# The last 512 weight columns of two heads loaded in unequal row groups

## The chip, the cores and the metric

The kernel runs on one core of one Trainium2 chip. The metric is the device time of one execution in microseconds (us). The core has the engines TensorE (PE), VectorE (DVE), ScalarE (ACT), GpSimd (POOL) and SyncE (SP), and 16 DMA engines, which carry all loads. TensorE's weight loads stand apart in the profile as PEld.

## The reference

Two layers, each an attention step over a key and value cache and a gated feed-forward, run twice with the same weights and caches. All is float32; two batch rows, one token each.

```python
def _A_ref(x, k_cache, v_cache, wq, wo):          # H 16, Sk 4096, Dh 256, D 448
    q = (x @ wq).reshape(B, Sq, H, Dh).transpose(0, 2, 1, 3)
    scores = jnp.einsum("bhqd,bhkd->bhqk", q, k_cache) * (Dh ** -0.5)
    p = _softmax(scores, axis=-1)
    o = jnp.einsum("bhqk,bhkd->bhqd", p, v_cache)
    return o.transpose(0, 2, 1, 3).reshape(B, Sq, H * Dh) @ wo
def _B_ref(x, W_gate, W_up, W_down):              # F 1792
    gate = jnp.einsum("bsd,df->bsf", x, W_gate)
    gate = gate * (gate > 0)
    return jnp.einsum("bsf,fd->bsd", gate * jnp.einsum("bsd,df->bsf", x, W_up), W_down)
x = x + _A_ref(_layernorm(x), ...); x = x + _B_ref(_layernorm(x), ...)
x = x + _A_ref(_layernorm(x), ...); x = x + _B_ref(_layernorm(x), ...)
```

## The kernel before

The work is a stream of loads from HBM into one large SBUF tile, the arena, with the arithmetic fitted beside it. A unit is one head of one batch row: 32 units in each of the two passes. Keys and values of a unit lie in HBM as rows of 128 partitions; a whole block is the values of one unit and the keys of the next, 128 rows of 16384 numbers, 64 KB each (8 MB in all). Beside them go the head weights (`in_w_head_dram`): for each head 128 rows of 1792 numbers (7 KB each). Of these columns the first 896 hold the query weights, and the last 896 the output weights, in two halves of 448 that the projection multiplies one after the other. After the 32 units of a pass come the feed-forward's weights (`in_w_in_dram`, `in_w_out_dram`), likewise in rows of 7 KB, and the very last of them in narrower pieces.

`loads` writes the order of all loads by hand, first for pass 1, then for pass 2, and `pending` holds it. `pump` (called at every `release` of a buffer) takes loads from the head of that list while there is room in the arena and issues each as one DMA from SP's queue (the page's line L142). The arena has three whole blocks and three single places; a head's weights go into a single place. `query(u)` multiplies a head's first 896 columns, `project(u)` the last 896 (PE, L579), and `project` then releases the head's place, for which the next head's load waits. In pass 2 the heads come in the order 15, 14, 0, 1, ... 13, so heads 9 and 11 are loaded late in pass 2, each between two whole blocks.

In the last feed-forward, `block` (PE, L736) multiplies by `in_w_out_dram` as it arrives, and the results are copied out by ACT and DVE (L762, L769, L777) and stored by two small DMAs.

A load with 128 rows is spread over the 16 DMA engines by rows. Each engine works through its own queue in order; nothing holds one engine back for another, unless an issue waits. What SP waits for before an issue is a buffer's release, and the semaphore of the load eight issues earlier, which the new load uses again (named DMAHW0 to DMAHW7 in the program). Instructions of the five engines are fetched by the same 16 DMA engines, in packets of 16 KB (queue q8) and 8 KB (queue q14).

## Time and profile before

| | |
|---|---|
| time, median of 3 runs (range) | 1317.86 us (1317.57 to 1317.97) |
| the profiled execution's own time | 1317.97 us |
| its span, first to last instruction | 1316.1 us |
| busy share of PE, DVE, ACT, POOL | 43%, 82%, 15%, 22% |
| loads on SP's queue | 99.5% of the 16 DMA engines' span |
| moved | 561.32 MB, mean 427 GB/s |
| mean granted TensorE clock | 0.686 |

In the tables of stretches, a row gives the stretch in us from the span's start, its length, each engine's busy time with its number of instructions, the granted TensorE clock, the busy share of the 16 DMA engines (1.00 is all sixteen) and GB/s. In a list of instructions in order of time a row gives start, duration, engine, line, operation, and in brackets the idle time before it with what ended it. In the list of waits a row names who waited for whom, then us in total, times, and the longest. A list of DMA queues gives packets, MB and the time that the packets took as a share of 16 engines over the stretch.

### The profile page before, as it was taken

What the parts mean: (1) busy time and instruction counts of PE and PEld (TensorE: products, weight loads), DVE (VectorE), ACT (ScalarE), POOL (GpSimd) and SP (SyncE); (2) the same over time, 40 slices, a digit from 0 to 9 for tenths busy, and PEclk for the clock granted to TensorE, in tenths of its full rate; (3) what the DMA queues carried; (4) which work ended last, traced back from release to release, by engine and by line L of the source; (5) the groups of instructions that cost most, each with busy time, mean ns of one, the idle gap of its engine ahead of it and who ended that gap; (6) DMA issues with size and microseconds to landing.
All of it is one profiled execution on the core that took longest, in us unless ns stands there. A gap on an engine that the chain in (4) does not pass through costs nothing.

```text
span 1316.1 us, 9097 instructions
## 1 busy us (share of the span) xinstructions
PE 561.0 (43%) x3280; PEld 194.9 (15%) x3280; DVE 1082.5 (82%) x789; ACT 198.2 (15%) x779; POOL 291.4 (22%) x192
## 2 busy tenths in 40 slices
PE   2243342433424334245495544232443424424358
PEld 2011110110111101112142111010111101111113
DVE  4989888898888988788829987698898888877892
ACT  1100000010000000221016523000000000012242
POOL 0202003322133221321001153022052321130210
PEclk9676766767667676676796667666666667666569
DMA  9999999999999999999999999999999999999998
GB/s 406 438 431 426 437 427 430 439 434 429 424 443 432 431 435 419 444 423 428 422 397 402 430 428 436 440 431 428 429 441 431 428 435 435 426 434 429 428 423 333
DMA packets 22665, 561.32 MB, mean 427 GB/s; under 512 B 2520, under 2 KB 2652, under 8 KB 9948
## 3 DMA queue, kind: packets, MB, share of 16 engines
q1 hardware_dynamic: 22612, 560.74, 99.5%
q8 instruction: 26, 0.43, 0.1%
q14 instruction: 19, 0.16, 0.0%
q10 hardware_dynamic: 8, 0.00, 0.0%
HBM read 560.73 MB, written 0.00 MB: 426 GB/s over the span
## 4 chain that ended last, share of the span: by engine, by line
DMA 56%; DVE 30%; PE 8%; POOL 2%; issue 2%; ACT 1%; DVEq 0%; SPq 0%; POOLq 0%; ACTq 0%
DMA arena<-in_vk_dram 53%; DVE arena L431 12%; DVE tiny L445 11%; PE po L530 2%; DVE down L477 2%; POOL tiny L488 2%; DMA arena<-in_w_in_dram 2%; DVE arena L468 2%; DVE arena L477 2%; DMA arena<-in_w_out_dram 1%; PE small L556 1%; DVE row L546 1%; PE acc L579 1%; PE pq L377 1%; ACT arena L470 1%
## 5 line engine op out<-in xcount | busy, mean ns | idle before, releaser
L431 DVE TENSOR_TENSOR arena<-arena 128x8192 f32<-128x8192 f32 (+2 forms) x52 | 441.8, 8497 | 108.0 <-DMA arena<-in_vk_dram 107.9
L445 DVE TENSOR_REDUCE tiny<-arena 128x32 f32<-128x8192 f32 (+2 forms) x53 | 430.3, 8118 | 0.0
L556 PE MATMUL small<-tiny,row 128*128 128x1 f32 x256 | 62.0, 346 | 667.1 <-DVE row L546 667.1
L530 PE MATMUL po<-arena,tiny 128*2 128x512 f32 x2052 | 303.5, 733 | 20.4 <-ACT arena L521 10.3
L488 POOL PARTITION_ALL_REDUCE tiny<-tiny x64 | 71.0, 1109 | 625.2 <-DVE tiny L486 625.2
L502 POOL PARTITION_ALL_REDUCE tiny<-tiny x64 | 192.1, 3002 | 61.3 <-ACT tiny L496 60.3
L556 PEld LDWEIGHTS small<-tiny,row 128*128 128x128 f32 x256 | 56.6, 308 | 728.2 <-DVE row L546 728.2
L493 ACT ACTIVATE tiny<-tiny 128x1 f32<-128x1 f32 x64 | 18.8, 294 | 600.9 <-POOL tiny L488 600.9
L393 POOL PARTITION_BROADCAST arena<-arena x58 | 27.6, 545 | 296.1 <-ACT arena L389 296.1
L530 PEld LDWEIGHTS po<-arena,tiny 128*2 128x2 f32 x2052 | 55.3, 96 | 209.4 <-issue 192.3
L377 PE MATMUL pq<-arena,xs 128*33 128x256 f32 x174 | 76.8, 611 | 12.6 <-DMA arena<-in_w_head_dram 12.6
L579 PE MATMUL acc<-arena,tiny 128*2 128x448 f32 x128 | 50.2, 881 | 32.1 <-DVE tiny L569 32.1
L389 ACT ACTIVATE arena<-pq 33x256 f32<-33x256 f32 x29 | 10.9, 377 | 318.7 <-PE pq L381 318.7
L437 ACT ACTIVATE arena<-arena 128x256 f32<-128x256 f32 x104 | 41.7, 402 | 87.7 <-DVE arena L431 87.7
L546 DVE SCALAR_TENSOR_TENSOR row<-po,tiny,row 128x256 f32<-128x256 f32 x64 | 30.7, 480 | 25.8 <-ACT row L543 25.5
L470 ACT ACTIVATE arena<-arena 128x256 f32<-128x256 f32 x117 | 47.1, 404 | 20.8 <-DVE arena L468 20.5
L468 DVE TENSOR_TENSOR arena<-arena 128x1024 f32<-128x1024 f32 (+1 forms) x24 | 42.0, 1749 | 0.0
L377 PEld LDWEIGHTS pq<-arena,xs 128*33 128x33 f32 x174 | 25.7, 164 | 79.5 <-issue 65.8
L543 ACT ACTIVATE row<-po,tiny 128x256 f32<-128x256 f32 x64 | 29.2, 456 | 27.3 <-PE po L530 27.2
L477 DVE SCALAR_TENSOR_TENSOR down<-arena,pq 128x256 f32<-128x256 f32 x64 | 26.9, 420 | 5.4 <-PE pq L356 3.4
L569 DVE TENSOR_TENSOR tiny<-small,tiny 128x4 f32<-128x4 f32 x32 | 5.2, 161 | 28.6 <-PE small L556 28.6
L496 ACT ACTIVATE tiny<-tiny 128x32 f32<-128x32 f32 x64 | 26.4, 413 | 2.1
(154 smaller groups left out, 372.6 us busy)
## 6 DMA issues: line engine op xcount, KB each, us to landing
arena<-in_vk_dram SPq DMA_DIRECT2D x16, 4096.0 KB, 40.2
arena<-in_w_head_dram SPq DMA_DIRECT2D x31, 896.0 KB, 30.9
arena<-in_vk_dram SPq DMA_DIRECT2D x12, 2048.0 KB, 38.7
arena<-in_vk_dram SPq DMA_DIRECT2D x24, 1024.0 KB, 16.4
arena<-in_w_in_dram SPq DMA_DIRECT2D x14, 896.0 KB, 26.2
arena<-in_vk_dram SPq DMA_DIRECT2D x1, 6784.0 KB, 40.1
arena<-in_w_out_dram SPq DMA_DIRECT2D x5, 896.0 KB, 9.0
arena<-in_vk_dram SPq DMA_DIRECT2D x3, 896.0 KB, 8.8
```

Source lines behind the costliest of these rows:

```text
L377: nc.tensor.matmul(q, xs[:, c, :], w[:, c * DH : (c + 1) * DH], start=(c == 0), stop=False)
L431: nc.vector.tensor_mul(part, part, q_of[u][:, None, :].to_broadcast([P, n, DH]))
L445: nc.vector.reduce_sum(found, part, axis=AX.X)
L468: nc.vector.tensor_mul(some, some, q_of[u][:, None, :].to_broadcast([P, whole, DH]))
L470: nc.scalar.activation(kt[:, t, :], kt[:, t, :], AF.Copy, accum_out=found[:, t : t + 1])
L477: nc.vector.scalar_tensor_tensor(junk if kept else kt[:, t, :], kt[:, t, :], 1.0, q_of[u], op0=ALU.mult, op1=ALU.mult, accum_out=found[:, ...
L488: nc.gpsimd.partition_all_reduce(mx_of[u], mx, P, RED.max)
L502: nc.gpsimd.partition_all_reduce(total[:, b : b + 1], rs, P, RED.add)
L530: nc.tensor.matmul(po_of[u][32 * t : 32 * t + 2, (i - 2 * t) * DH : (j - 2 * t) * DH], p_of[u][:, n : n + 2], values[:, i * DH : j * DH], ...
L546: nc.vector.scalar_tensor_tensor(row[:, :DH], po_of.pop(u)[:, DH:], lead[:, 1:2], row[:, :DH], op0=ALU.mult, op1=ALU.add,)
L556: nc.tensor.matmul(pT_of[u - u % 2][:, c, b : b + 1], row[:, c * P : (c + 1) * P], ones, start=True, stop=True,)
L579: nc.tensor.matmul(acc[at : at + B], oT_of[h][:, c, :], wo[:, c * D : (c + 1) * D], start=(n < 3), stop=(n >= n_u - 3),)
```

## The change

When the weights of head 9 and of head 11 are loaded for the second time (pass 2), the load is issued as three DMAs instead of one: the first 1280 columns in all 128 rows, and then the last 512 columns (2 KB a row) in two groups of rows. For head 9 these are rows 0 to 119 and rows 120 to 127, for head 11 rows 0 to 103 and rows 104 to 127. Bytes, places in the arena and all arithmetic stay as they were; pass 1 and the other heads too.

```diff
+SHARED = {9: 120, 11: 104}
+WIDE = 512
...
+    loaded = set()
...
-            for i, j in zip(parts, parts[1:]):
-                nc.sync.dma_start(dst[:, i:j], src[:, i:j])
+            shares = [(slice(0, P), i, j) for i, j in zip(parts, parts[1:])]
+            if kind == "h" and name in SHARED and name in loaded:
+                many, few = SHARED[name], F - WIDE
+                shares = [(slice(0, P), 0, few)]
+                shares += [(rows, few, F) for rows in (slice(0, many), slice(many, P))]
+            if kind == "h":
+                loaded.add(name)
+            for rows, i, j in shares:
+                nc.sync.dma_start(dst[rows, i:j], src[rows, i:j])
```

SP's queue late in pass 2, before the change: the loads of heads 9, 10 and 11 (`in_w_head_dram`), with two whole blocks between them.

```order
120 L142 DMA arena<-in_w_head_dram 128x1792 [waits PE_49,Activation_49,Pool_49]
121 L142 DMA arena<-in_vk_dram 128x16384 [waits DMAHW5_49,DVE_49,PE_49]
122 L142 DMA arena<-in_vk_dram 128x16384 [waits DMAHW3_49,DMAHW7_49,DVE_49,PE_49]
123 L142 DMA arena<-in_w_head_dram 128x1792 [waits PE_49,Activation_49,Pool_49]
124 L142 DMA arena<-in_vk_dram 128x16384 [waits DMAHW0_49,DVE_49,PE_49]
125 L142 DMA arena<-in_vk_dram 128x16384 [waits DMAHW2_49,DMAHW6_49,DVE_49,PE_49]
126 L142 DMA arena<-in_w_head_dram 128x1792 [waits PE_49,Activation_49,Pool_49]
```

The same place of SP's queue after the change.

```order
120 L152 DMA arena<-in_w_head_dram 128x1280 [waits PE_49,Activation_49,Pool_49]
121 L152 DMA arena<-in_w_head_dram 120x512 [waits PE_49]
122 L152 DMA arena<-in_w_head_dram 8x512 [waits DMAHW3_49]
123 L152 DMA arena<-in_vk_dram 128x16384 [waits DMAHW5_49,DVE_49,PE_49]
124 L152 DMA arena<-in_vk_dram 128x16384 [waits DMAHW7_49,DVE_49,PE_49]
125 L152 DMA arena<-in_w_head_dram 128x1792 [waits PE_49,DMAHW6_49,Activation_49,Pool_49]
126 L152 DMA arena<-in_vk_dram 128x16384 [waits DMAHW0_49,DVE_49,PE_49]
127 L152 DMA arena<-in_vk_dram 128x16384 [waits DMAHW4_49,DVE_49,PE_49]
128 L152 DMA arena<-in_w_head_dram 128x1280 [waits PE_49,DMAHW1_49,Activation_49,Pool_49]
129 L152 DMA arena<-in_w_head_dram 104x512 [waits DMAHW2_49,PE_49]
130 L152 DMA arena<-in_w_head_dram 24x512 [waits DMAHW3_49]
```

Two issues more stand at each of the two heads, ahead of the next whole block, and every later load has another semaphore. On PE only the projection of such a head is another: its first multiplication waits for the two small loads as well.

```order
487 L566 MATMUL small<-tiny,row 128x1 [waits DVE_49]
488 L566 MATMUL small<-tiny,row 128x1
489 L589 MATMUL acc<-arena,tiny 2x448 [waits DMAHW3_49,DMAHW2_49,DVE_49]
490 L589 MATMUL acc<-arena,tiny 2x448
491 L387 MATMUL pq<-arena,xs 33x256 [waits DMAHW1_49,PE_49,Pool_49]
```

Before the change the row numbered 489 waits for DVE alone. No instruction of PE, DVE, ACT or POOL changes its place.

## Prediction

> **What bounds the kernel now.** I read the profile page first (its span, its DMA queues and its chain of waits), then the chain near the end, then stretches of the span for the share of DMA engines at work.

> ```profile
> span 1316.1 us, 9097 instructions
> DMA packets 22665, 561.32 MB, mean 427 GB/s; under 512 B 2520, under 2 KB 2652, under 8 KB 9948
> q1 hardware_dynamic: 22612, 560.74, 99.5%
> q8 instruction: 26, 0.43, 0.1%
> q14 instruction: 19, 0.16, 0.0%
> DMA 56%; DVE 30%; PE 8%; POOL 2%; issue 2%; ACT 1%; DVEq 0%; SPq 0%; POOLq 0%; ACTq 0%
> ```

> SP's loads (q1) keep the 16 DMA engines 99.5% busy, so bytes over engines set the time: 427 GB/s is 26.7 GB/s for one engine. How loads are dealt to the engines is seen in the count. There are 157 loads of 128 rows; 128 row packets and 16 small ones (under 512 B, an engine's report that its share is done) make 144 for each, and 157 x 144 = 22608, four short of the 22612, which the store of two rows at the end leaves. So each load puts 8 rows on each of 16 engines. The 26 instruction packets of q8 (0.43 MB, 16 KB each) and the 19 of q14 are not dealt so: each falls whole on one engine and makes that one late. This is why the engines don't end together.

> The chain near the end, and then stretches of the span:

> ```profile
> 1298.66 13.88 DMA arena<-in_w_out_dram
> 1312.54 0.04 issue
> 1312.59 0.47 PE spare L736 x18
> ```

> ```profile
> 0.00:400.00 400.00, 147.88 (x800) 51.63 (x804) 339.56 (x116) 35.09 (x107) 81.21 (x60) 0.68 1.00 431
> 1306.00:1307.00 1.00, 1.00 (x7) 0.18 (x3) 0.00 (x0) 0.00 (x0) 0.00 (x0) 1.00 0.99 398
> 1307.00:1308.00 1.00, 0.90 (x4) 0.27 (x3) 0.62 (x1) 0.00 (x0) 0.00 (x0) 1.00 0.89 353
> 1308.00:1309.00 1.00, 0.92 (x13) 0.39 (x15) 0.65 (x3) 0.29 (x2) 0.00 (x0) 1.00 0.65 258
> 1309.00:1310.00 1.00, 1.00 (x40) 1.00 (x42) 0.41 (x4) 0.14 (x1) 0.00 (x0) 1.00 0.53 206
> 1310.60:1311.70 1.10, 0.84 (x24) 0.38 (x17) 0.00 (x0) 0.28 (x1) 0.00 (x0) 1.00 0.25 97
> 1311.80:1311.86 0.06, 0.06 (x4) 0.06 (x8) 0.00 (x0) 0.00 (x0) 0.00 (x0) 1.00 0.14 51
> 1312.03:1312.40 0.37, 0.37 (x14) 0.10 (x3) 0.00 (x0) 0.00 (x0) 0.00 (x0) 1.00 0.06 22
> ```

> The end hangs on the last pieces of the feed-forward's weights, and these on the last engine. With no load left to issue, the share falls from 0.99 after 1306 us to 0.25 in 1310.60 to 1311.70: four engines of 16 are still at work, the other twelve are done by 1310.60. By 1311.80 one of the four or two have gone (0.14), and from 1312.03 to 1312.40 a single one is left (0.06 is 1/16). Against the last engine, the other three of this group are 0.37 to 0.70 us early (1312.40 less 1312.03, and less 1311.70), and all others at least 1.80 us.

> An engine's lateness carries over from load to load, since each works through its own queue; relief given at 1045 us still counts at 1312 us, unless all run dry between.

> **The change part by part.** *The bytes.* A row of 512 columns is 2048 B, at 26.7 GB/s 0.077 us; 8 rows are 0.61 us. Before, each engine has 8 such rows of each of the two heads, 16 in all. How 120, 8, 104 and 24 rows are dealt no row of this trace shows. The nearest one below is the load of x with 2 rows, alone on queue q10 in this stretch:

> ```profile
> DMA packets 5, 0.01 MB, mean 31 GB/s; under 512 B 2, under 2 KB 4, under 8 KB 5
> q10 hardware_dynamic: 4, 0.00, 2.9%
> ```

> (1.40 to 1.75 us.) Two rows leave two reports: two engines, a row each. Between 2 rows on 2 engines and 128 on 16, I take equal whole rows on the most engines, the same engines first each time: 120 = 15 x 8, 8 = 8 x 1, 104 = 13 x 8, 24 = 12 x 2. Then eight engines have 8 + 1 + 8 + 2 = 19 rows (+3, +0.23 us), four have 18 (+0.15), one 16 (0), two 8 (-0.61) and one none (-1.23); 152 + 72 + 16 + 16 = 256, as before. [...] The other end, 120 rows still on 16 engines, would spare none: 0.

> *More packets.* A row in two pieces costs a start more. The nearest prices are stretches of 64 KB and of 7 KB rows:

> ```profile
> 326.00:358.00 32.00, 13.67 (x70) 4.72 (x74) 28.43 (x9) 1.54 (x5) 7.62 (x5) 0.61 0.99 428
> 1290.00:1297.00 7.00, 6.53 (x38) 1.86 (x36) 0.65 (x2) 1.39 (x4) 0.00 (x0) 1.00 1.01 418
> ```

> 7168 B at 418/16 GB/s are 274 ns, at 428/16 268: 6 ns a row. 16 rows split (8 for each head) make at most 0.10 us on an engine; I take 0.05, from 0 to 0.15 with the reports.

> *Four issues more on SP.* SP's issues around heads 9 and 11, and its waits there:

> ```profile
> 1044.85 0.33 SPq L142 DMA_DIRECT2D arena<-in_w_head_dram  x1
> 1051.70 20.75 SPq L142 DMA_DIRECT2D arena<-in_vk_dram  x2
> 1085.75 0.33 SPq L142 DMA_DIRECT2D arena<-in_w_head_dram  x1
> 1126.63 0.33 SPq L142 DMA_DIRECT2D arena<-in_w_head_dram  x1
> SPq L142 <- DVE tiny L445: 77.1, 6, 20.0
> SPq L142 <- PE acc L579: 39.7, 3, 13.2
> ```

> An issue takes 0.33 us. After head 9 (1044.85) the next block is issued at 1051.70, a wait of 6.5 us for DVE; two issues, 0.66 us, lie inside it: 0. Queued behind them on SP is that block's issue, for which DVE's next product waits; but the DMA engines have some 30 us of work before they reach it, since a head lands 31 us after its issue.

> ```profile
> arena<-in_w_head_dram SPq DMA_DIRECT2D x1, 896.0 KB, 30.9
> ```

> (326 to 358 us.) The new waits on DMAHW semaphores are for the load eight issues earlier, more than one block back in the queue; it has landed when two blocks of 20 us each have been waited for. 0, at worst a wait of under 1 us in that cover.

> *The projection's wait.* The last columns are read when the head is projected, and that frees its place for the third load after it (three places; heads are issued every 41 us: 1044.85, 1085.75, 1126.63). So the reading comes some 120 us after the issue, the landing 31 us after it. 0.

> *The tail.* If loads end earlier, PE must be able to follow. Its three waits for them at the end:

> ```profile
> 1310.79 0.38 PEld L736 LDWEIGHTS po<-arena,row 128*32 128x32 f32 x16 [0.18 <-DMA arena<-in_w_out_dram]
> 1311.77 0.52 PE L736 MATMUL po<-arena,row 128*32 128x128 f32 x10 [0.33 <-DMA arena<-in_w_out_dram]
> 1312.59 0.47 PE L736 MATMUL spare<-arena,row 128*32 128x64 f32 x18 [0.18 <-DMA arena<-in_w_out_dram]
> ```

> 0.18 + 0.33 + 0.18 = 0.69 us can be handed on; beyond that PE is the bound.

> *Sum.* The trace doesn't number the engines, so which of them are the last four is my choice, and the sign hangs on it. I take the group of four that ends by itself to be a block of neighbours, and the three spared engines to be in it with the very last among them. The spared then end at least 0.98 us earlier (0.37 + 0.61, or 1.23), and the fourth is the last: 0.6 us ahead of the old end (within 0.37 to 0.70), less 0 to 0.23 for its own added rows and 0.05 for packets. That is -0.4 us (-0.1 to -0.7). 1317.97 - 0.4 = 1317.57; the median lies 0.11 under the profiled execution: 1317.5.

> **The rivals.** (1) *The last engine is not one of the spared.* It then has up to three rows more and the packets: +0.05 to +0.4, taken as +0.25: 1318.1. For it: 13 of 16 engines are not spared. Against it: only a lone last engine with the three spared ones all outside would do it.

> (2) *Slower: engines in each other's way.* In 128-row loads every engine writes its own 8 partitions. With 15 or 13 engines at 8 rows the borders shift, and an engine writes partitions that are another's in the load beside it; the engines are up to 5 us apart, so the other is writing there. If a group of partitions takes in no more than one engine's 26.7 GB/s, both halve for that time: the writer loses up to 0.61 us a head and the owner as much, 2.45 us for both heads, more for the small groups. An engine that was spared 0.61 or 1.23 keeps less, so the end moves by +0.6 to +2.8, in the middle +1.6: 1319.4. It decides once the loss passes 0.4 us, a sixth of the full price. For it: the rate of 26.7 is one for all row sizes, as a shared way in would give. Against it: x's two rows went to partitions 0 and 1 by two engines at once, and the four packets took 2.9% of 16 engines in 0.35 us, 0.16 us, 0.08 a row, where 1792 B alone at 26.7 GB/s are 0.067; no halving, though of a tiny load. [...]

> (3) *The rows are not dealt so.* If 120 and 104 rows fall on few engines, these become last: all 256 rows on four engines are 64 each, 4.9 us less the 1.23 of before, +3.7 (1321.6); on one, some 13 to 18 us. Against it: two rows found two engines.

> (4) *Everything evens out.* The idle engine time after 1306 us, from the shares above, is 0.01 + 0.11 + 0.35 + 0.47 and some 1.9 for the last 2.4 us, 2.8 us an engine. Only all of it would be a gain over 0.2% (2.64 us, about what a measurement of this kernel can tell from no change).

> **How the numbers follow.** Forecast 0.42, rival 1 0.15, rival 2 0.33, rival 3 0.07, rival 4 0.03. Forecast, rival 1 and three quarters of rival 2 (0.25, up to +2.6) lie within 0.2%: 0.82. Slower: the rest of rival 2 (0.08) and rival 3, 0.15. Faster: 0.03. Range: from 1317.0 (the forecast's -0.7 and a run's scatter of 0.2) to 1320.0 (rival 2 up to +2.1); outside are rivals 3 and 4 and the top of rival 2, under 0.2.

> **What would show it.** Right: the share stays at 0.25 for a shorter time before the last load lands, the span ends 0.4 us sooner, the packets of q1 rise by 256 rows and the reports (to 22612 + 256 + 15 + 8 + 13 + 12 = 22916), and SP's waits keep their releasers. Rival 1: the single engine's stretch lasts longer. Rival 2: while heads 9 and 11 land, row packets take longer and the DMA share stays near 1.00 with fewer GB/s. Rival 3: other counts of reports. The forecast is wrong if the last load lands later than 1312.5 us.

## The result and the profile after

The change makes the kernel a little slower.

| | before | after |
|---|---|---|
| median (range) | 1317.71 us (1316.79 to 1318.14, 10 runs) | 1320.88 us (1320.26 to 1321.87, 10 runs) |
| ratio, 95% interval | 1 | 1.0027 [1.0019, 1.0035] |
| profiled execution, own time and span | 1317.97 and 1316.1 us | 1321.35 and 1319.6 us |

That is +3.17 us, where the forecast was 1317.5 us; it lies beyond the upper end of the range (1320.0). In the three fences that follow stand lines of the page of after, its chain near the end, and its last stretches.

```profile
span 1319.6 us, 9104 instructions
DMA packets 22969, 561.33 MB, mean 425 GB/s; under 512 B 2568, under 2 KB 2700, under 8 KB 10252
q1 hardware_dynamic: 22916, 560.74, 99.4%
```

```profile
1302.21 13.60 DMA arena<-in_w_out_dram
1315.80 0.04 issue
1315.85 0.47 PE spare L746 x18
```

```profile
1311.00:1312.00 1.00, 0.89 (x9) 0.52 (x9) 0.36 (x2) 0.00 (x0) 0.00 (x0) 1.00 0.76 300
1313.00:1314.00 1.00, 1.00 (x40) 1.00 (x34) 0.00 (x0) 0.28 (x1) 0.00 (x0) 1.00 0.49 184
1315.00:1316.00 1.00, 0.80 (x25) 0.52 (x29) 0.00 (x0) 0.28 (x1) 0.00 (x0) 1.00 0.05 19
```

The kernel still ends on the last engine's last weights, and the same work follows: the last load lands at 1315.80 us instead of 1312.54, 3.26 of the span's 3.5 us. The loads on q1 carry the same bytes at the same share (99.4%), in the 22916 packets that were forecast. The tail still thins out engine by engine, over some 5 us. So most of the loss was brought there from further up.

It arose at two places. The first two fences compare the DMA queues of before and of after in 15 us around the landing of head 9 (1065 to 1080 us); the third is from the 45 us ahead of it (1000 to 1045 us), where the two executions show the same line.

```profile
DMA packets 247, 6.57 MB, mean 438 GB/s; under 512 B 32, under 2 KB 32, under 8 KB 160
```

```profile
DMA packets 386, 5.78 MB, mean 386 GB/s; under 512 B 55, under 2 KB 55, under 8 KB 311
```

```profile
DMA packets 461, 19.60 MB, mean 435 GB/s; under 512 B 48, under 2 KB 48, under 8 KB 176
```

While head 9 lands, 0.79 MB less are moved in the same time; at the mean of 427 GB/s of before these are 1.85 us. Around head 11 (1147 to 1162 us) it is 371 GB/s where before had 446. Single microseconds at head 9, first of before and then of after, show how (a packet counts in the microsecond in which it starts, so that a share can pass 1.00):

```profile
1073.00:1074.00 1.00, 0.00 (x0) 0.00 (x0) 0.42 (x1) 0.89 (x4) 0.34 (x1) 1.00 1.02 434
```

```profile
1072.00:1073.00 1.00, 0.00 (x0) 0.00 (x0) 0.10 (x1) 0.39 (x2) 0.35 (x1) 1.00 1.36 390
1073.00:1074.00 1.00, 0.00 (x0) 0.00 (x0) 0.00 (x0) 0.77 (x3) 0.38 (x1) 1.00 0.97 275
1074.00:1075.00 1.00, 0.00 (x0) 0.00 (x0) 0.90 (x1) 0.00 (x0) 0.00 (x0) 1.00 0.97 286
```

The DMA engines are all at work (0.97), yet move 275 GB/s instead of 434: busy and slow, the mark that the prediction named for rival 2. The packet records of after show the same in single packets. The 2 KB rows at head 9 take 121 ns in the median and up to 178, where an undisturbed one takes 84, and 64 KB rows of the blocks beside them take up to 3.59 us instead of 2.42. Over all packets there an engine loses 1.86 us on average at head 9 and 1.74 at head 11. Both sides lose, but not alike: of the 1.86 us the 2 KB rows make 0.28, the 5 KB rows of the same head 0.34, and the 64 KB rows of the whole blocks 1.22. So what the text ahead of the prediction says, that nothing holds one engine back for another unless an issue waits, does not hold here: with the engines at work (0.97), the 64 KB rows took up to 3.59 us.

SP's queue in after, in order of time:

```profile
1044.69 1.19 SPq L152 DMA_DIRECT2D arena<-in_w_head_dram  x3
1051.71 0.36 SPq L152 DMA_DIRECT2D arena<-in_vk_dram  x1
```

Three issues take 1.19 us and end at 1045.88; the next block is issued at 1051.71, where before had 1051.70. The added issues, 0.86 us more than the 0.33 of before, cost nothing there.

### The profile page after: what moved, and what is told of

It is laid out like the page before. It is cut to its first block, busy times and chain, and to the rows that moved or that the text cites. A ratio compares the mean times of both kernels' runs of the same rounds, so it can differ in the third digit from the quotient of the medians.

```text
span 1319.6 us, 9104 instructions
## 1 busy us (share of the span) xinstructions
PE 560.0 (42%) x3280; PEld 194.4 (15%) x3280; DVE 1082.5 (82%) x789; ACT 198.4 (15%) x779; POOL 265.1 (20%) x192
## 3 DMA queue, kind: packets, MB, share of 16 engines
q1 hardware_dynamic: 22916, 560.74, 99.4%
## 4 chain that ended last, share of the span: by engine, by line
DMA 56%; DVE 29%; PE 9%; POOL 2%; issue 2%; ACT 1%; SPq 0%; DVEq 0%; POOLq 0%; ACTq 0%
DMA arena<-in_vk_dram 53%; DVE arena L441 12%; DVE tiny L455 9%; PE po L540 3%; DVE down L487 2%; POOL tiny L498 2%; DMA arena<-in_w_in_dram 2%; DVE arena L478 2%; DVE arena L487 2%; PE pq L387 1%; PE acc L589 1%; DMA arena<-in_w_out_dram 1%; DVE row L556 1%; PE small L566 1%; ACT arena L480 1%
## 5 line engine op out<-in xcount | busy, mean ns | idle before, releaser
L498 POOL PARTITION_ALL_REDUCE tiny<-tiny x64 | 71.0, 1109 | 626.5 <-DVE tiny L496 626.5
L512 POOL PARTITION_ALL_REDUCE tiny<-tiny x64 | 165.8, 2591 | 61.3 <-ACT tiny L506 61.3
L579 DVE TENSOR_TENSOR tiny<-small,tiny 128x4 f32<-128x4 f32 x32 | 5.2, 162 | 28.6 <-PE small L566 28.6
## 6 DMA issues: line engine op xcount, KB each, us to landing
arena<-in_w_head_dram SPq DMA_DIRECT2D x29, 896.0 KB, 30.9
arena<-in_w_in_dram SPq DMA_DIRECT2D x14, 896.0 KB, 24.8
arena<-in_w_out_dram SPq DMA_DIRECT2D x5, 896.0 KB, 17.4
arena<-in_vk_dram SPq DMA_DIRECT2D x3, 896.0 KB, 8.5
```

Of the source, the lines that this page charges most:

```text
L498: nc.gpsimd.partition_all_reduce(mx_of[u], mx, P, RED.max)
L512: nc.gpsimd.partition_all_reduce(total[:, b : b + 1], rs, P, RED.add)
```

## The experiments

The theory is that the engines get in each other's way on the side of SBUF, since rows are dealt so that an engine writes where another engine writes at that time. Its rivals are these: the load in three parts costs by itself (packets, reports, issues); the uneven dealing makes an engine late; the place in HBM does it. The letters of the theories in the expectations are set anew from run to run. Times are compared with runs of before on the same chip: its medians were 1317.24 (first four), 1317.41 (next four) and 1317.43 us (last four).

**The split by columns alone.** The last 512 columns are a load of their own, in all 128 rows.

```diff
-                shares += [(rows, few, F) for rows in (slice(0, many), slice(many, P))]
+                shares += [(rows, few, F) for rows in (slice(0, P),)]
```

> The two heads' loads are split by columns alone: 128 rows of 1280 and 128 rows of 512 columns, so every engine keeps its 8 rows of each. Theory A (engines get into each other's way where one writes partitions that another engine serves): nothing crosses a border, so the time of before within 0.2 us, and 2 KB packets of 84 to 90 ns. Theory B (more loads, packets and reports cost): about half of the 3.2 us or more, +1.5 us.

Measured: 1317.67 us, ratio 1.0002 [0.9993, 1.0011]. Its DMA queues from 1065 to 1080 us:

```profile
DMA packets 388, 6.42 MB, mean 428 GB/s; under 512 B 48, under 2 KB 48, under 8 KB 304
```

There are as many packets as in after (388, there 386), at 428 GB/s where after has 386. Splitting by columns, with its packets and reports, costs nothing that could be measured; what costs is the split by rows.

**Even dealing, shifted rows.** 112 and 16 rows at both heads; if equal rows go to all 16 engines, every engine has 8 rows again, as 7 and 1.

```diff
-SHARED = {9: 120, 11: 104}
+SHARED = {9: 112, 11: 112}
```

> Rows 0 to 111 and 112 to 127 for both heads. Both numbers divide by 16, so every engine again has 8 rows in all (7 and 1), as before the change; only which rows it has is shifted. Theory A: as slow as the changed kernel, +2.5 to +4 us, with 2 KB packets of 110 ns and more. Theory C (the cost comes from the uneven dealing, engines with nothing or more to do): the time of before within 0.3 us.

Measured: 1320.73 us, ratio 1.0029 [1.0019, 1.0040]. From 1065 to 1080 us:

```profile
DMA packets 393, 5.65 MB, mean 377 GB/s; under 512 B 64, under 2 KB 64, under 8 KB 320
```

The 64 reports (under 512 B) are 32 more than those of before, 16 for each of the two added loads: both go to all 16 engines. That each engine has 7 and 1 rows of them is the author's estimate; by it the full loss comes without any unevenness in the number of rows. Neither relief nor added rows explain it.

**Other rows of HBM.** All 128 rows again, but read from eight rows further on in HBM, written to the same partitions.

```diff
...
+                    part = every[name * P + 8 : name * P + 8 + P, i:j]
```

> Split by columns as in the first kernel, but the 512 columns are read from rows 8 further on in HBM, so that each engine reads other rows while it writes its own partitions (the last columns of the two heads then hold wrong numbers). Theory A with the clash at the SBUF side: the time of before within 0.2 us. Theory D (the clash is where HBM is read): +2 to +3 us.

Measured: 1317.97 us, ratio 1.0005 [0.9996, 1.0014]; 425 GB/s in the same stretch. So an engine that reads eight rows further on, and writes where it always does, loses nothing: by this it isn't the reading side.

**Twice the columns.** `WIDE = 1024` instead of 512.

> As the changed kernel, but the last 1024 columns instead of 512 go in the uneven groups: the same loads, row groups and reports, twice the bytes in them. Theory A, cost by bytes: about twice the cost, +5.5 to +6.5 us against before. Theory B or C with a cost for each load or report: +3.2 us as with 512.

Measured: 1323.62 us, ratio 1.0051 [1.0037, 1.0065]: +6.4 us, twice the loss. From 1065 to 1080 us:

```profile
DMA packets 378, 5.26 MB, mean 351 GB/s; under 512 B 55, under 2 KB 55, under 8 KB 311
```

Twice the bytes in the same loads cost twice as much: the price goes by bytes, not by loads or reports.

**Which engines.** Before, with tiny loads of n rows of 4n bytes into a spare tile beside heads 5 to 8 and 10 (twelve loads, where the text below says thirteen).

```diff
+MARKS = {5: (8, 4, 12), 6: (15, 14, 13), 7: (6, 10), 8: (9, 11), 10: (3, 7)}
...
+                    nc.sync.dma_start(marks[:k, col : col + k], w_head[name][:k, :k])
```

> The kernel before with thirteen tiny loads of n rows (n from 3 to 15, of n numbers each, 12 to 60 B a row, none of 5) set beside the loads of heads 4 to 10 in pass 2, into a spare tile. If n rows go to the n lowest engines, the packets in an engine's queue tell its number, and so which engines are the last ones at the end. The forecast had engines 12 to 15 as the last four; the other reading has them spread. Time as before within 0.5 us, since the loads hold under 4 KB in all.

Measured: 1317.9 us, ratio 1.0005 [0.9995, 1.0015]. From its page:

```profile
q1 hardware_dynamic: 22836, 560.74, 99.5%
```

22836 is 22612 + 224, and the rows of the twelve loads add up to 112: each row is a packet and has a report, so n rows went to n engines for each of the twelve n (3, 4 and 6 to 15). That these are the lowest in number, as the text above supposes, was not shown. The engines could not be followed from the marks to the end of the program, so this run does not name the last four. In the packet records of after, the one engine with no 2 KB row at head 9 (its report follows a 5 KB row and is followed by a 64 KB row) starts on the next whole block at 1071.81 us, the second of the sixteen, which start between 1071.73 and 1076.75: it is not a late one. It loses all the same: its next two 64 KB rows take 3.59 and 3.04 us instead of 2.42, 1.8 us more.

**64 and 64 rows.** `SHARED = {9: 64, 11: 64}`. An engine's own partitions are, in the text below, the 8 that it writes in a load of 128 rows, with rows taken as dealt in order.

> Rows 0 to 63 and 64 to 127 for both heads: 16 engines with 4 rows of each. [...] If its own partitions are 8 neighbours, only 2 of 16 engines keep theirs: the full cost, +2.7 to +3.5 us. [...]

Measured: 1321.07 us, ratio 1.0027 [1.0016, 1.0037]: full cost, +3.7 us. Eight neighbours as a group forecast the full cost (+3.5 at most).

**Head 9 alone.** `SHARED = {9: 120}`.

> Only head 9 in uneven groups (120 and 8 rows). The cost of each head stands for itself: +1.6 to +2.0 us, by the changed kernel's trace. If the two heads work together (the second meets engines that the first has pushed out of step), under +1.2.

Measured: 1319.18 us, ratio 1.0009 [1.0000, 1.0018], +1.8 us. The block issued after head 9, and then the one issued after head 11, us from issue to landing:

```profile
arena<-in_vk_dram SPq DMA_DIRECT2D x1, 45.0
```

```profile
arena<-in_vk_dram SPq DMA_DIRECT2D x1, 43.2
```

In before it took 43.4 us after head 9, in after 45.1. So head 9 costs its half of the loss by itself; head 11 alone was not run.

**Without the small groups.** The loads of 8 and of 24 rows are left out, so that an eighth of the bytes isn't loaded.

```diff
-                shares += [(rows, few, F) for rows in (slice(0, many), slice(many, P))]
+                shares += [(rows, few, F) for rows in (slice(0, many),)]
```

> As the changed kernel, but the loads of 8 and of 24 rows are left out (these rows keep older numbers, so the two heads' last columns are wrong there). They hold an eighth of the bytes. If the cost goes by the bytes that cross: +2.5 to +3.0 us. If the small groups make it (8 engines on the last 8 partitions at once): under +1.5.

Measured: 1320.45 us, ratio 1.0024 [1.0014, 1.0034], +3.0 us: the large groups do it. This speaks against one reading of "its own partitions": if an engine served eight neighbouring partitions, 120 rows dealt in order, eight to an engine, would leave each engine at home. The last four runs look at which partitions belong together. In them theory A is that eight neighbours are a group; theory B that four neighbours and the four that lie 32 further are one; theory C that any load of fewer than 128 rows costs, whichever partitions it writes. All three are the author's suppositions, for these runs to decide on.

**Even rows and odd rows.** 64 and 64 again, but as every second row.

```diff
-... for rows in (slice(0, many), slice(many, P))]
+... for rows in (slice(0, P, 2), slice(1, P, 2))]
```

> For heads 9 and 11 in pass 2 the last 512 columns come in two loads of 64 rows, the even rows and then the odd ones (instead of the first 64 and the last 64, which took 1.0027 times the time before). Row counts, packets and issues are the same as there; only which partitions fall to which engine differs: dealt in order, four to an engine, engine e gets the even and then the odd ones of partitions 8e to 8e + 7. Theory A (a group is eight neighbouring partitions, and an engine's own in a 128-row load): no engine leaves its own group, no cost, 1317.5. Theory B (a group is four neighbours and the four that lie 32 further): most engines leave their own, full cost, +2.5 to +3.5: 1320 to 1321. Theory C (every load of fewer than 128 rows beside whole blocks costs, whichever partitions it writes): +2.5 to +3.5 too.

Measured: 1317.6 us, ratio 1.0002 [0.9993, 1.0011]. From 1065 to 1080 us in the run with the first 64 and the last 64 rows, and then in this one:

```profile
DMA packets 395, 5.78 MB, mean 386 GB/s; under 512 B 64, under 2 KB 64, under 8 KB 320
```

```profile
DMA packets 405, 6.44 MB, mean 429 GB/s; under 512 B 64, under 2 KB 64, under 8 KB 320
```

The loads, row counts and packet sizes are the same; only which rows stand in which load differs, and the whole loss is gone. That a load has fewer than 128 rows (theory C) is not the cause.

**Eight rows, 1, 4 and 8 apart.** At six heads four loads of 8 rows each, a row to each of eight engines (the 64 reports in the fences below are the 32 of before and four times 8); the step between the rows is all that differs among the three runs. The other 96 rows of these columns are left out, so that with no loss a run is faster than before (by the expectation, 1315.7 to 1316.9 us).

```diff
+SHARED = {3: 8, 5: 8, 7: 8, 9: 8, 11: 8, 13: 8}
+STEP = 4
...
+... (slice(k * many if STEP == 1 else k, (k * many if STEP == 1 else k) + 7 * STEP + 1, STEP) for k in range(4))]
```

> For six heads of pass 2 (3, 5, 7, 9, 11, 13) the last 512 columns are loaded in 32 rows only, in four loads of 8 rows (8 engines, a row each): here rows 0 to 7, 8 to 15, 16 to 23, 24 to 31. The other 96 rows of these columns are left out, so that the arena keeps what stood there. Without any clash the 8 engines save 4 rows of 0.077 us at each head, 1.85 us in all, the others 3.7 us; PE can follow by 0.69 us at the end: 1315.7 to 1316.9. Theory A (groups of eight neighbours): all eight engines write into one group at once, so each load takes up to 0.61 us instead of 0.077, four of them 2.45 us instead of 0.31, at most +12.9 us for the six heads if all arrive together; as they are up to 5 us apart, a third of it, +4. Theory B (four neighbours and the four 32 further): two groups for eight engines, at most +5.5, a third +1.8. Theory C: the same for the three steps.

> As with step 1, the rows taken 4 apart: rows 0, 4, ... 28, then 1, 5, ... 29, and so on; the same 32 rows, 96 left out. Theory A: four groups of eight neighbours, two engines in each: at most +1.9, a third +0.6. Theory B: eight groups for eight engines, none shared among themselves: least of the three steps, 1315.7 to 1316.9 if these are also the engines' own groups. Theory C: the same as with step 1.

> As with step 1, the rows taken 8 apart: rows 0, 8, ... 56, then 1, 9, ... 57, and so on, 32 rows of the first 64; 96 left out. Theory A: each engine writes a row of its own group: no cost, 1315.7 to 1316.9, least of the three steps. Theory B: four groups (partitions 0 and 32 share one), two engines in each: at most +1.9, a third +0.6. Theory C: the same as with step 1.

Measured: step 1 1318.19 us, 1.0008 [0.9999, 1.0017]; step 4 1315.31 us, 0.9989 [0.9980, 0.9998]; step 8 1318.42 us, 1.0008 [0.9999, 1.0018]. The DMA queues around head 9 (1065 to 1080 us) for the steps 1, 4 and 8 in turn:

```profile
DMA packets 307, 6.16 MB, mean 411 GB/s; under 512 B 64, under 2 KB 64, under 8 KB 224
```

```profile
DMA packets 311, 6.42 MB, mean 428 GB/s; under 512 B 64, under 2 KB 64, under 8 KB 224
```

```profile
DMA packets 308, 6.23 MB, mean 415 GB/s; under 512 B 64, under 2 KB 64, under 8 KB 224
```

B's forecast for even and odd rows (full cost) was wrong, which came from what it added: that 64 rows are dealt in order, four to an engine. B holds with both results if an even and an odd half of each such group go to the same engine. The three runs write no partition above 59; carried on to all 128 by the author's estimate, B has 16 groups, of which the first 64 rows reach only 8, with 16 engines at work, and 120, 112 or 104 rows cut two, four or six of the groups in half. How 128, 120 or 104 rows are dealt in row numbers was not seen. So it is shown that the choice of rows decides (386 GB/s for the first 64 and the last 64 rows, 429 for even and odd ones), and at 8 rows the step between them (411, 428 and 415 GB/s); that engines crowd the same groups, at 120 and 104 rows too, is argued, and stays open.

## Why the prediction was wrong

What held: 120, 8, 104 and 24 rows go to 15, 8, 13 and 12 engines as taken (22916 packets, as forecast to the packet; around heads 9 and 11 the reports without the small groups are 47 and 45, which is 32 + 15 and 32 + 13, and with them 55 and 57, 8 and 12 more). The issues on SP are hidden in its wait, the next block after head 9 was not issued later (1051.71 for 1051.70 us), and more packets cost nothing that shows (split by columns: 1.0002). The bound was read rightly: loads, and at the end the last engine.

What failed is the step that put the clash of engines at nothing: the forecast's sum has terms for relief, added rows and packets, and none for engines that slow each other. The runs showed 1.86 and 1.74 us lost on an engine at the two heads in its place.

- *The choice between forecast and rival 2.* Rival 2 is what happened, by its own sign (busy engines, fewer GB/s). It had a chance of 0.33, the forecast 0.42. The row that tipped it was x's load: two rows of 1792 B written at once with no halving to be seen (72 ns each, from 1.66 us). These are 3.6 KB, and the trace shows no packet of another load until they have landed (the first at 1.75 us); here 256 KB a head run beside blocks of 64 KB rows. A free result at that size is no bound for the other.
- *The price of rival 2.* It was put at 0.61 us for the writer and as much for the owner, at each head, less what a spared engine gains: +1.6 in the middle, +2.8 at most, and the range was cut inside that, at +2.1. The writer's part was less than that, 0.28 us at head 9, and the part of the rows beside was more, 1.56 (0.34 on 5 KB rows and 1.22 on 64 KB rows). Even the engine spared at head 9 loses 1.8 us there, more than the 0.61 us that it is spared. The measured +3.17 us is near the sum of the two heads, 3.6.
- *Whom it spares.* The forecast's sign hung on the last engine being among the three spared. The one engine that is spared at head 9 is not a late one there. Which engines are last was not settled, but with 112 and 16 rows, where none is spared, costing as much, the answer would hardly have changed the sign. The sum has a slip here besides: an end at least 0.98 us earlier for all three holds only if the very last engine is the one spared at both heads; spared at one, it gains 0.61.
- *"Its own 8 partitions" as neighbours.* Rival 2's picture of shifted borders gave the right sign, but by luck in its reason: if groups were eight neighbours, 120 rows, eight to an engine, would cross no border, and yet the two large groups alone cost +3.0 us.

## What to carry to other kernels

When the DMA engines are full, as here, a load that goes beside others is by these runs best split by columns, in all 128 rows: that was free (1.0002), while the contiguous row groups slowed the loads in flight, in proportion to their bytes (+3.2 us with 512 columns, +6.4 with 1024). If rows must be split, try groups that reach all the partitions evenly (even and odd rows cost nothing here, the first and the last 64 rows 3.7 us). Giving a late engine's rows to others is no gain by itself: here the engine spared at head 9 lost more to the clash (1.8 us) than the rows that it was spared (0.61).

## What was not expected of the hardware

The DMA share of a profile does not show this loss: in the single microseconds above it is 0.97 or more while the rate falls from 434 to 275 GB/s, and over the whole kernel it is 99.4% for 99.5%. Only the rate, or the time of one packet, shows it. And the loss is larger than the rows that cause it: the 256 KB of a head are on average 8 rows of 0.077 us for each engine (2048 B at 427/16 GB/s), 0.61 us, and cost each some 1.8 us (1.86 and 1.74). Why it is three times as much was not tried.
